# The head of a retention kernel, rewritten by half chunks, with more weight loads issued ahead

## The chip, the cores and the metric

The kernel runs on one core of a Trainium2 chip. The time is device microseconds of one launch. The core's engines run beside each other, each its own instructions in their written order: TensorE (PE, matrix products), VectorE (DVE), ScalarE (ACT), GpSimd (POOL, idle here) and SyncE (SP), which issues DMAs.

## The reference

```python
scores = scale * np.matmul(q, k.transpose(0, 1, 3, 2))      # 4 batches, 8 heads, 576 tokens, 64 wide
gamma = 1.0 - 2.0 ** (-5.0 - np.arange(H, dtype=np.float32))
Dmat = np.where(rel >= 0, gamma[:, None, None] ** rel[None, :, :], 0.0)
x = np.matmul(scores * Dmat[None, :, :, :], v)              # then to 2304 tokens x 512
h = x @ w_in;  g = np.maximum(h, 0) + np.log1p(np.exp(-np.abs(h)));  x = g @ w_out     # 512 -> 2048 -> 512
h = x @ w2_in; r = np.maximum(h, 0); out = (r * r) @ w2_out
```

All in float32. The decay is split into factors of the key's token (multiplied into v) and of the query's token (the table xw, multiplied into the result), so that only a triangular mask of zeros and ones is left, and everything before a chunk is one 64x64 state per head.

## The kernel before, in words

**Chunks.** The 2304 tokens are 18 chunks of 128, each two half chunks of 64 tokens; 9 half chunks are one batch, and the state begins anew with each batch. Per half chunk: scores k times q, a mask, the output from the masked scores and from the carried state, and the state's own sum.

**Layers.** The two matrix layers work on tiles of 512 or 384 tokens. Each weight matrix of the first pair is cut into 16 slices of 128 hidden units ("wi" of w_in, "wo" of w_out). A raw slice (512 KB, loaded into one of three stage buffers by `load_w`) is turned into words (`words`: two ScalarE instructions, L152 and L153, then two of VectorE, L157 and L160) and split into a high part (ScalarE's cast, L188) and a low part (VectorE's subtraction, L189). A product is three passes: high by high, low by high, high by low. `pump_load(upto)` issues loads up to a number, `pump_begin` starts slices, `pump_end` finishes them one step later.

**The head.** Lines 1136 to 1219 are written in an order by hand ("manual schedule"), and each engine keeps it. They compute attention for the first four chunks (tile 0), the factor tables xw for half chunks 1 to 8 (sent as one row, spread by TensorE in `spread_rows`, multiplied by VectorE in `make_xw` and by ScalarE in `scalar_xw`, four instructions per half chunk), and the first weight slices. In the kernel before, a chunk's queries and keys come in two loads, heads 0 to 3 into partitions 0 to 63 and heads 4 to 7 into the others (`early_qk`), and both half chunks are worked on together, over 128 tokens: `early_scores` makes 128x128 scores, `early_mask` masks 1024 columns, `early_states` adds all 128 tokens, and one copy of the state (`kept`) carries it to the next chunk. `early_x` multiplies by xw (x), and ScalarE's cast and `early_low` split x. `early_g1` is the first-layer product of slice 0 in two column halves. Slice 0 is finished in the head; slices 1 and 2 have their words made there and are split in step 0.

**The steps after it.** Step j does the first-layer product of slice j (L515), softplus, one visit of the attention (`visit`: scores L391, states L416, outputs L439, masks L401, the scaling of v L372), the split of its result (L533, L534), the second-layer product of slice j-2 (L549), and starts two more slices. The visits of steps 0 and 1 are scores alone: chunk 3 was finished by the head, and the first half of chunk 4 is the last of its batch, whose state nobody needs. Step 2 begins with outputs that need the mask of step 1, step 3 with states that need the values scaled in step 2. Attention chunks from the fifth on sit in a ring of two buffers (`ring`), loaded as whole rows of 4 KB in all 128 partitions.

**Warming.** `keep_warm(n)` gives TensorE n products of zeros, of two instructions each.

## Time and profile before

| | |
|---|---|
| median of 3 runs | 826.17 us (826.15 to 827.8) |
| the profiled execution | 823.74 us |
| its span, first to last instruction | 822.0 us |
| mean granted TensorE clock | 0.997 |
| busy: TensorE, VectorE, ScalarE | 810.8 (99%), 607.2 (74%), 378.9 us (46%) |
| DMA | 189.37 MB, mean 230 GB/s |

The profile has a page with busy times, forty slices, DMA queues and the chain that ended last, and views of the trace behind it: windows (busy time in stretches), the chain of waits, timelines of one engine, and DMA issues with their time to landing. "Idle before" is the time an engine stood before an instruction, followed by what released it. A product in float32 is recorded as two instructions. In a timeline neighbouring instructions of one kind are one row.

### The profile page before, as it was taken

The page shows a single profiled execution, that of the slowest core. Times are in us where ns is not written, and L with a number is a line of the kernel's source. Part 1 is how long each engine was busy: PE and PEld are TensorE (multiplying, and loading weights), DVE is VectorE, ACT ScalarE, POOL GpSimd, SP SyncE. Part 2 cuts the span into 40 slices and gives each one's busy share as a digit, 9 for nine tenths or more (in the row PEclk, how much of TensorE's full clock was granted, in tenths as well). Part 3 has the DMA queues.
Part 4 walks back from the last instruction along what each step waited for, and adds up shares of the span by engine and source line. Part 5 has one row for each costly group of instructions (what it writes and reads, how often), then busy time and mean ns, then how long its engine had stood idle before and what let it go on. Part 6 is the DMA issues. An engine that isn't in the chain of part 4 may idle for free.

```text
span 822.0 us, 16243 instructions
## 1 busy us (share of the span) xinstructions
PE 810.8 (99%) x5957; PEld 721.6 (88%) x5957; DVE 607.2 (74%) x1160; ACT 378.9 (46%) x739; POOL 0.2 (0%) x4
## 2 busy tenths in 40 slices
PE   8898999999999999999999999999999999999998
PEld 5777999988888888888999999988999988999887
DVE  4998766646565664646796498998798997787876
ACT  3787666535344543545665221454211554111553
POOL 0000000000000000000000000000000000000000
PEclk9999999999999999999999999999999999999999
DMA  9967554466666655656979387898978889888885
GB/s 238 310 219 239 180 180 124 134 207 215 209 229 213 194 172 188 197 181 211 300 251 300 94 251 248 271 297 285 299 249 254 250 271 282 282 249 249 251 274 170
DMA packets 122802, 189.37 MB, mean 230 GB/s; under 512 B 10466, under 2 KB 68450, under 8 KB 122722
## 3 DMA queue, kind: packets, MB, share of 16 engines
q1 hardware_dynamic: 122560, 188.26, 72.1%
q8 instruction: 47, 0.77, 0.4%
q14 instruction: 31, 0.25, 0.1%
q10 hardware_dynamic: 164, 0.09, 0.1%
HBM read 147.41 MB, written 40.89 MB: 229 GB/s over the span
## 4 chain that ended last, share of the span: by engine, by line
PE 95%; DMA 3%; DVE 1%; ACT 0%; SPq 0%; issue 0%; DVEq 0%; ACTq 0%
PE acc L549 24%; PE ph L515 24%; PE py L685 9%; PE py L758 9%; PE px L685 6%; PE pz L758 6%; PE px L758 6%; PE pz L685 6%; PE po L439 2%; DMA qk<-in_qk_t_dram 1%; PE pb L391 1%; PE st L416 1%; DMA kv<-in_kv_dram 1%; DMA ring<-in_qk_t_dram 1%; SPq L970 0%
## 5 line engine op out<-in xcount | busy, mean ns | idle before, releaser
L515 PE MATMUL ph<-xh,wi 128*128 128x512 f32 (+1 forms) x632 | 144.4, 370 | 1.3 <-DVE wi L189 0.8
L515 PEld LDWEIGHTS ph<-xh,wi 128*128 128x128 f32 x632 | 115.9, 189 | 17.0 <-DVE wi L189 1.2
L549 PE MATMUL acc<-gh,woh 128*128 128x512 f32 (+1 forms) x320 | 120.5, 377 | 0.0
L549 PE MATMUL acc<-gh,wol 128*128 128x512 f32 (+1 forms) x320 | 117.8, 368 | 0.0
L549 PE MATMUL acc<-gl,woh 128*128 128x512 f32 (+1 forms) x320 | 117.8, 368 | 0.0
L534 DVE TENSOR_TENSOR gl<-e,gh 128x512 fp32r<-128x512 f32 (+1 forms) x80 | 51.0, 637 | 71.1 <-ACT gh L533 70.3
L526 ACT ACTIVATE e<-ph 128x512 f32<-128x512 f32 (+1 forms) x80 | 44.3, 554 | 126.4 <-PE ph L515 126.2
L685 PE MATMUL py<-t,sring 128*128 128x384 f32 x432 | 88.3, 338 | 0.0
L515 PE MATMUL ph<-xl,wi 128*128 128x512 f32 (+1 forms) x316 | 78.2, 369 | 0.0
L685 PEld LDWEIGHTS py<-t,sring 128*128 128x128 f32 x432 | 74.8, 188 | 2.5 <-DVE uring L889 0.5
L549 PEld LDWEIGHTS acc<-gh,woh 128*128 128x128 f32 x320 | 60.0, 188 | 8.6
L549 PEld LDWEIGHTS acc<-gh,wol 128*128 128x128 f32 x320 | 60.1, 188 | 7.7
L549 PEld LDWEIGHTS acc<-gl,woh 128*128 128x128 f32 x320 | 60.1, 188 | 6.9
L515 PEld LDWEIGHTS ph<-xl,wi 128*128 128x128 f32 x316 | 58.5, 190 | 7.6
L738 ACT CAST gh<-g 128x384 fp32r<-128x384 f32 x84 | 43.2, 515 | 46.2 <-PE px L758 16.1
L738 ACT CAST gring<-g 128x384 fp32r<-128x384 f32 x84 | 43.2, 515 | 39.9 <-PE py L758 16.2
L685 PE MATMUL pz<-t,sring 128*128 128x384 f32 x288 | 58.3, 334 | 0.0
L685 PE MATMUL px<-t,sring 128*128 128x384 f32 x288 | 58.0, 335 | 0.0
L401 DVE TENSOR_TENSOR ring<-pb,cst 64x256 f32<-64x256 f32 x56 | 23.6, 422 | 44.1 <-PE pb L391 27.2
L706 DVE TENSOR_TENSOR g<-g 128x384 f32<-128x384 f32 x96 | 52.6, 554 | 1.5
L706 DVE TENSOR_TENSOR gring<-g,gring 128x384 fp32r<-128x384 f32 x84 | 46.2, 553 | 9.5 <-ACT gring L738 8.3
L706 DVE TENSOR_TENSOR gl<-g,gh 128x384 fp32r<-128x384 f32 x84 | 46.5, 554 | 8.8 <-ACT gh L738 7.7
(123 smaller groups left out, 1403.2 us busy)
## 6 DMA issues: line engine op xcount, KB each, us to landing
sring<-s2d SPq DMA_DIRECT2D x168, 256.0 KB, 3.1
sring<-o2d SPq DMA_DIRECT2D x168, 256.0 KB, 3.2
wi_raw<-in_moe_w_in_dram SPq DMA_DIRECT2D x32, 512.0 KB, 4.9
wo_raw<-in_moe_w_out_dram SPq DMA_DIRECT2D x32, 512.0 KB, 4.1
s2d<-ct SPq DMA_DIRECT2D x48, 256.0 KB, 2.8
o2d<-ct SPq DMA_DIRECT2D x48, 256.0 KB, 3.4
ring<-in_qk_t_dram SPq DMA_DIRECT2D x14, 512.0 KB, 4.1
ring<-in_kv_dram SPq DMA_DIRECT2D x14, 512.0 KB, 6.3
```

The lines of the kernel that those rows point to most:

```text
L391: nc.tensor.matmul(pb[to, h, :], lhsT=kk[:, hh, :], rhs=qp[:, hh, :], start=True, stop=True, skip_group_check=True,)
L401: nc.vector.tensor_tensor(out=chunk[c][rows, 1, i * HH:(i + 1) * HH], in0=pb[of], in1=mask[of], op=ALU.mult)
L416: nc.tensor.matmul(st[to, h, :], lhsT=kk[:, hh, :], rhs=sv[:, hh, :], start=m == h == 0, stop=True, skip_group_check=True,)
L439: nc.tensor.matmul(po[(LO, HI)[hh % 2], hh // 2, :], lhsT=before[rows, hh, :] if carried else sv[:, hh, :], rhs=qp[:, hh, :] if carried el ...
L515: nc.tensor.matmul(ph[:, :n], lhsT=a, rhs=x, start=(j == 0), stop=(j == len(todo) - 1))
L526: nc.scalar.activation(out=g, in_=hps.pop(key)[:, :n], func=AF.Softplus)
L534: nc.vector.tensor_tensor(out=l[:, :n], in0=g, in1=h[:, :n], op=ALU.subtract)
L549: nc.tensor.matmul(acc[j][:, :n], lhsT=a, rhs=x, start=(begin and m == 0), stop=(end and m == 2))
L685: nc.tensor.matmul(ps, lhsT=a, rhs=x, start=(first and m == 0), stop=(m == len(todo) - 1), skip_group_check=True,)
L706: nc.vector.tensor_tensor(out=out, in0=a, in1=b, op=ALU.subtract)
L738: nc.scalar.copy(h, src)
L758: nc.tensor.matmul(blocks[m][:, :cols], lhsT=a[:, c], rhs=x, start=(first and p == n == 0), stop=(p == NP - 1 and n == len(todo) - 1), ski ...
```

## The change

The head is written anew. Queries and keys of the first four chunks come like those of the ring, as whole rows of 4 KB in all partitions, one load per pair (q and k; k and v). Scores, states and outputs are made per half chunk, by the functions that the later visits use; scores and masks cover 64x64 blocks, so a chunk's mask has 512 columns. The state is carried after each half chunk, by `next_state`, into one of two buffers. The table rows move from ScalarE's to SyncE's DMA queue. The warming products are two, not six, and the single one after `spread_rows` goes. Weight slice 0 is loaded before chunks 2 and 3, and three more raw slices get buffers of their own (`ahead`, in the place of a later slice group), so that six are loaded in the head. Slice 1 is split in the head; slice 2's words are made there.

```diff
+EXTRA = 3
+    ahead = wts.tile([P, EXTRA, DM, 2], U32, tag="wi2", name="ahead")
     def load_w(src, kind, f):
-        t = stage.tile([P, DM, 2], U32, tag="st", name=f"{kind}_raw")
+        if STAGES <= n_load[0] < STAGES + EXTRA:
+            t = ahead[:, n_load[0] - STAGES]
+        else:
+            t = stage.tile([P, DM, 2], U32, tag="st", name=f"{kind}_raw")
...
     def pump_load(upto):
+        if upto >= STAGES:
+            upto = min(upto + EXTRA, max(2 * STAGES + EXTRA, upto))
...
+    def early_load(c, i):
+        if c not in chunk:
+            chunk[c] = first_pool.tile([P, 4, H, CN], F32, tag=f"chunk{c}", name="chunk", bufs=1)
+        nc.sync.dma_start(
+            out=chunk[c][:, i:i + 2],
+            in_=(qk_t, None, kv)[i][2 * c:2 * c + 2].rearrange("s p i h c -> (s p) i h c"),
+        )
     def early_scores(c):
+        pb = ps_head.tile([P, H, CN], F32, tag="pb", name="pb", bufs=2)
+        for hh in range(H):
+            for rows in (LO, HI):
+                nc.tensor.matmul(
+                    pb[rows, hh, :], lhsT=chunk[c][rows, 1, hh, :], rhs=chunk[c][rows, 0, hh, :],
+                    start=True, stop=True, skip_group_check=True,
+                )
+        return pb
+    def early_mask(c, pb):
+        nc.vector.tensor_tensor(out=chunk[c][:, 1], in0=pb, in1=whole_mask, op=ALU.mult)
+    carried = [
+        first_pool.tile([P, H, CN], F32, tag=f"carried{i}", name="carried", bufs=1)
+        for i in range(2)
+    ] * (last // 2) + [before]
+    def early_state(c, s):
+        for fn in states(c, s):
+            fn()
+    def early_next(c, s):
+        next_state(c, s, carried[c + s])
+    def early_outputs(c):
+        po = pos[c] = ps_head.tile([P, 2, 512], F32, tag="po", name="po", bufs=1)
+        both = (
+            outputs(c, s, po[:, s].rearrange("p (a n) -> p a n", n=CN), False, carried[c])
+            for s in range(2)
+        )
+        rounds(*(at_rounds((0, fns)) for fns in both))
...
+        early_load(0, 0)
         for half in (LO, HI):
             nc.scalar.dma_start(out=cst[half, :C_XW], in_=consts[CN:P, :C_XW])
+        early_load(0, 2)
+            nc.sync.dma_start(out=rows_in[r:r + 1], in_=consts[r:r + 1, C_XW:])
+        early_load(1, 0)
+        early_load(1, 2)
+        pump_load(1)
+        early_load(2, 0)
+        early_load(2, 2)
+        early_load(3, 0)
+        early_load(3, 2)
+        for _ in range(2):
+            load_w(*loads[n_load[0]])
+            n_load[0] += 1
         load_chunk(last)
+        pump_load(STAGES)
-        keep_warm(6)
+        keep_warm(2)
+        pb0 = early_scores(0)
+        scale_v(0)
+        early_mask(0, pb0)
+        early_state(0, 0)
+        early_next(0, 0)
+        pb1 = early_scores(1)
+        scale_v(1)
+        early_state(0, 1)
+        early_mask(1, pb1)
+        early_next(0, 1)
         spread_rows()
-        keep_warm(1)
...
+        early_state(1, 1)
+        early_next(1, 1)
+        make_xw(2, 2)
+        scalar_xw(4)
+        early_x(0)
+        pb2 = early_scores(2)
+        scale_v(2)
+        early_mask(2, pb2)
+        early_state(2, 0)
+        early_next(2, 0)
+        scalar_xw(5)
+        early_low(0)
+        early_outputs(1)
+        early_state(2, 1)
+        early_next(2, 1)
+        scalar_xw(6)
+        words0 = begin_words()
+        scale_v(3)
+        early_keep(0)
+        pb3 = early_scores(3)
+        early_x(1)
+        early_state(3, 0)
+        early_next(3, 0)
+        scalar_xw(7)
+        early_mask(3, pb3)
+        next(words0)
+        early_outputs(2)
+        early_state(3, 1)
+        early_x(2)
+        early_low(1)
+        early_keep(1)
+        next(words0)
+        early_outputs(3)
+        early_x(3)
+        early_low(2)
+        early_keep(2)
+        early_next(3, 1)
+        scalar_xw(8)
+        words1 = begin_words()
+        early_low(3)
+        early_keep(3)
         early_g1(0)
+        next(words1)
+        next(words1)
+        words2 = begin_words()
+        next(words2)
```

## Rows read from the trace of the kernel before

**Rows 1.** The page, part 4: shares of the span on the chain that ended last.
```profile
PE 95%; DMA 3%; DVE 1%; ACT 0%; SPq 0%; issue 0%; DVEq 0%; ACTq 0%
```

**Rows 2.** Chain of waits, 0 to 60 us: start, length, what (us).
```profile
9.58 9.78 DMA qk<-in_qk_t_dram
...
31.64 4.38 PE ph L515 x11
```

**Rows 3.** Windows: stretch, its length, busy us (instructions) by engine, TensorE's clock, DMA share, GB/s.
```profile
7.00:8.00 1.00, 1.00 (x4) 0.38 (x2) 0.00 (x0) 0.00 (x0) 0.00 (x0) 1.00 1.12 208
...
24.00:25.00 1.00, 1.00 (x24) 0.85 (x16) 0.90 (x3) 0.19 (x2) 0.00 (x0) 1.00 1.05 402
...
0.00:26.00 26.00, 22.46 (x329) 14.66 (x330) 14.85 (x29) 11.92 (x33) 0.20 (x4) 1.00 0.97 266
...
2.00:4.00 2.00, 2.00 (x3) 0.67 (x2) 0.19 (x1) 0.97 (x1) 0.00 (x0) 1.00 0.80 211
...
30.00:35.00 5.00, 3.86 (x10) 2.87 (x11) 4.65 (x9) 2.80 (x5) 0.00 (x0) 0.72 0.94 315
```

**Rows 4.** Timeline of TensorE, 28 to 47 us: start, us, instruction, [idle before, releaser].
```profile
29.20 0.68 PE L391 MATMUL pb<-ring 64*64 64x64 f32 x16
...
30.29 0.50 PE L515 MATMUL ph<-xh,wi 128*128 128x512 f32 x1 [0.41 <-ACT wi L188]
...
31.64 2.94 PE L515 MATMUL ph<-xh,wi 128*128 128x512 f32 x7 [0.85 <-DVE wi L189]
...
34.37 1.65 PE L515 MATMUL ph<-xl,wi 128*128 128x512 f32 x4
...
38.52 1.07 PE L515 MATMUL ph<-xl,wi 128*128 128x512 f32 x4
...
39.51 0.27 PE L439 MATMUL po<-ring 64*64 64x64 f32 x2
...
46.40 0.27 PE L416 MATMUL st<-ring 64*64 64x64 f32 x2
```

**Rows 5.** DMA issues at 17.8 and 31.4 us: KB each, us from issue to landing.
```profile
ring<-in_kv_dram SPq DMA_DIRECT2D x1, 512.0 KB, 10.1
...
ring<-in_qk_t_dram SPq DMA_DIRECT2D x1, 512.0 KB, 6.4
```

**Rows 6.** Timeline of SyncE's queue, 14 to 18.5 us.
```profile
17.77 0.77 SPq L362 DMA_DIRECT2D ring<-in_kv_dram  x1
```

**Rows 7.** Timeline of VectorE, 9 to 45 us.
```profile
9.65 1.22 DVE L1013 TENSOR_TENSOR mixed<-pb,causal 128x1024 f32<-128x1024 f32 x1 [3.97 <-PE pb L992]
...
25.59 0.69 DVE L189 TENSOR_TENSOR wi<-ct,wi 128x512 fp32r<-128x512 f32 x1
...
28.18 0.69 DVE L157 SCALAR_TENSOR_TENSOR wi_raw<-wi_raw 128x512 f32<-128x512 f32 x1
...
28.90 0.69 DVE L160 SCALAR_TENSOR_TENSOR ct<-wi_raw 128x512 uint32<-128x512 uint32 x1
...
32.38 0.86 DVE L401 TENSOR_TENSOR ring<-pb,cst 64x256 f32<-64x256 f32 x2
...
36.68 0.86 DVE L401 TENSOR_TENSOR ring<-pb,cst 64x256 f32<-64x256 f32 x2
...
44.29 0.68 DVE L372 TENSOR_TENSOR ring<-ring,vw 128x512 f32<-128x512 f32 x1
```

**Rows 8.** Timeline of ScalarE, 19 to 28 us.
```profile
19.58 2.02 ACT L1131 ACTIVATE cst<-cst,times 128x64 f32<-128x64 f32 x8
...
24.94 0.62 ACT L188 CAST wi<-ct 128x512 fp32r<-128x512 f32 x1 [0.81 <-DVE ct L160]
...
25.46 0.69 ACT L152 ACTIVATE wi_raw<-wi_raw 128x512 f32<-128x512 f32 x1
...
26.04 0.75 ACT L153 ACTIVATE wi_raw<-wi_raw,cst 128x512 uint32<-128x512 uint16 x1
...
27.44 0.74 ACT L427 COPY ring<-st 64x256 f32<-64x256 f32 x2
```

## Prediction, made before the changed kernel had run

> **What bounds the kernel now.** I read the page first: the chain that ended last is 95% TensorE [rows 1], so over the whole span only what delays TensorE counts. The change touches the first 35 us alone, so the next view was the chain of that stretch. Until 19.4 us it is input DMA (the fourth query-key load was issued at 9.58 and took 9.78 us to land) [rows 2]. The windows say why: in 7 to 8 us, where almost only query-key halves move, DMA gave 208 GB/s; in 24 to 25 us, where a chunk is loaded as whole rows, 402 GB/s [rows 3]. From 30 to 35 us VectorE is busy 4.65 of 5 us, and TensorE stands twice (0.41 and 0.85 us) for the high and low parts of weight slice 1, then runs at a mean granted clock of 0.72 [rows 3, 4]. [...] So the head ends where VectorE and ScalarE have prepared weight slices 1 and 2 and the attention masks of steps 0 to 2. When TensorE restarts, and how far VectorE runs ahead of it then, decides. All later work is the same in both kernels, in the same order, and nothing in it waits for a fixed time, so a shift there reaches the end.

> **Input DMA (gain).** Up to and with the third chunk's key-value rows, the new order has seven loads of 524 KB (one weight slice among them), 69 KB of constants and 18 KB of factor rows: 3.76 MB. All but the weight slice and the factor rows now spread over 128 partitions in 4 KB rows. Bounds for their rate are 208 GB/s (halves) and 402 (whole rows); the nearest row is the whole-row one, and I take 380. Bytes begin to move at about 2.3 us (211 GB/s over 2 to 4 us is 0.42 MB) [rows 3]. A landing lags its last byte: 26.0 us at 266 GB/s make the 6.92 MB up to and with the first ring chunk's key-value rows, which were issued at 17.77 and took 10.1, so landed at 27.9; I take 1.8 us [rows 3, 5, 6]. Third chunk's key-value: 2.3 + 3.76/0.38 + 1.8 = 14.0 us; fourth, 1.05 MB later, 16.8. In the old kernel even the fourth query-key load came at 19.36 [rows 2]. At 300 GB/s the 14.0 becomes 16.6, at 402 it becomes 13.5, at 208 22.2.

> **What VectorE loses.** Masks of 128x1024 (1.22 us each) become 128x512; by the 128x512 products of other lines 0.68 each [rows 7], so four times 0.54, 2.2 us less. Scaling, the tables and the weight words cost what they did.

> **What ScalarE gains.** Each chunk now carries its state twice, in two 64x256 copies (0.74 a carry) [rows 8]. Seven carries come into the head, 5.2 us, for three single copies, which by the same row can't be under 0.37 each: some 4 us more. And the carries are serial: a state is added to only when it is copied out.

> **The sum: a serial chain on two engines.** From the third chunk on, each engine's next instruction waits for the other's. ScalarE's instructions overlap by 0.1 (starts 25.46 and 26.04, the first 0.69 long), so I count a carry 0.65, four factor tables 1.0 (2.02 for eight), a slice's words 1.25 (0.69 + 0.75), a cast 0.52, each 0.1 more where VectorE waits for its end [rows 8]; VectorE's words of a slice are 1.45, its subtraction or product 0.69 [rows 7].
> - 14.0, scaling 0.68, states 0.68 as eight 64x64 products on TensorE [rows 4]: 15.4.
> - ScalarE, without a gap: carry, tables of block 5, carry, tables 6, words of slice 0, cast of x1, carry, tables 7: 0.65+1.0+0.65+1.0+1.25+0.52+0.65+1.0 = 6.7: 22.1.
> - Cast of x2 0.52 and of slice 0 0.62; VectorE's low part 0.69 and x3 0.68: 24.6.
> - ScalarE: cast of x3 0.52, last carry 0.65, tables 8 1.0, words of slice 1 1.35: 28.1. VectorE's words 1.45: 29.6.
> - ScalarE: cast of slice 1 0.52, words of slice 2 1.35; VectorE's words 1.45; cast 0.62; low part 0.69: 34.2.
> - A dozen hand-overs at 0.05 (a cast of 0.62 that began at 24.94 released VectorE at 25.59) [rows 7, 8]: 34.8.

> There VectorE begins the mask of step 0, which stands at 32.38 in the old kernel [rows 7]: 2.4 us later, although its input came earlier. The old order gave ScalarE the words of slices 1 and 2 while VectorE still had x work of its own; the new one leaves VectorE idle at nearly every link (some 6 us in all).

> TensorE had room for part of this. The outputs of step 2 began at 39.51 and need the mask of step 1, which ended at 37.54; 2.4 later is 39.94: 0.4 us late. The states of step 3 began at 46.40 and need values scaled by 44.97; 2.4 later is 47.4, against 46.8: 0.6 more [rows 4, 7]. From there TensorE has no gap to give back. Sum so far: **+1.0 us**.

> **The clock.** Six warming products become two, and the one between goes too. The warming ran at three instructions in 2 to 4 us and at four in 7 to 8 alone [rows 3], so at half speed at first. The new TensorE ends warming near 4 us, does 0.7 us of scores and then stands until the first values are scaled, near 8. What the clock does then no row of before shows; the nearest is 30 to 35 us, where gaps of 0.41 and 0.85 us were followed by half speed (four products 1.65 us against 1.07) [rows 3, 4]. If states, scores and outputs run at half speed from 8 to 12 us, the second carry of chunk 1 and the tables behind it come up to 2.5 us late, of which the wait for the third chunk covers part. Bounds 0 and 2.5; I take +0.5. Later, TensorE stands about 2.9 us before slice 1 is ready (its restart falls near 31.4). The half-speed product that follows lies beside VectorE's lateness; what comes out past 40 us costs 0 to 1.5 (the loss of the old dip: 4.38 us times 1 - 1.07/1.65) [rows 2, 4]; I take +0.5.

> [...]

> **Six loads ahead.** They bring the first second-layer slice earlier, which VectorE's lateness covers anyway: 0. The loads after them, and the fifth ring chunk behind these on SyncE's queue, wait until slice 2's words are done (near 33.1): issue 33.5, landing near 40 with the 6.4 us that its query-key rows took before [rows 5], wanted just after 39.9. I take 0, bounds 0 and 0.5. Factor rows on SyncE's queue cost a microsecond of issue while a megabyte is queued: 0. The distance of the later loads stays.

> **Forecast.** +1.0 +0.5 +0.5 = +2.0 us. The profiled execution took 823.74 (span 822.0) and would take 825.7; the median of the runs shown, 826.17, stands 2.43 above it, so I predict **828.2**. About 0.2% (1.65 us) can be told from no change.

> **Rivals.**
> - *Half speed through the whole head.* [...] States, scores and outputs then take twice their time: 2.5 us up to the third chunk's first carry, 0.6 at the second, 0.9 at the last outputs, 4.0 on top of +1.0: 831.2. Chance 0.16.
> - *No clock cost, input at 402 GB/s.* The chain starts at 13.5, step 0's mask at 34.3: by the same two slacks TensorE is 0.5 late, 826.7, not to be told from no change. Chance 0.32.
> - *Faster: VectorE's saved work decides, not ScalarE.* If ScalarE is done before VectorE asks at each step, VectorE runs densely from the fourth chunk's landing: eight products and subtractions (5.5), three slices' words (4.35), two more low parts (1.4) and hand-overs (0.4), 16.8 + 11.6 = 28.4, 4.0 earlier than 32.38. TensorE then loses its gaps (1.26) and the dip (1.5): -2.8, 823.4. It decides from the point where ScalarE's 6.7 us end before 20 us; by the sum they end at 22.1. Chance 0.10.
> - The forecast itself, slower by 1.7 to 4 us: 0.42.

> Faster 0.10, same 0.32, slower 0.42 + 0.16 = 0.58. Range: below, the second rival with 0.9 of slack in my hand-overs and overlaps (825.8); above, the clock rival and half a microsecond for the ring chunk (831.8), which also holds a landing at 300 GB/s. The likeliest's own range is 827.8 to 830.2.

> **What would show it.** In the new trace: key-value landings near 14 and 17 us and DMA above 350 GB/s before 15 us (input); ScalarE without idle time from 15.5 to 22, and VectorE idle for about 2 us before the words of slice 1 (chain); step 0's mask on VectorE at 34 to 36; TensorE idle for about 3 us before the second first-layer product, released by the low part of slice 1; a granted clock below 1 between 8 and 12 us and again between 30 and 40. I am wrong if slice 1 is ready before 30 us, if the landings are as late as before, or if TensorE's outputs of step 2 begin before 39.51 [rows 4].

## The result and the profile after

The changed kernel takes 831.52 us (median of 4 runs, 830.85 to 831.88), the kernel before 826.78 beside it: a ratio of 1.0055 with a 95% interval of 1.0038 to 1.0073, some 4.7 us slower. The forecast was 828.2: the sign is right, the time lies at the upper end of the range, and the loss is more than twice what I gave it. The profiled execution took 831.65 us with a span of 829.8.

Kernels are compared by ratios, since the median of the kernel before moved between 826.0 and 827.7 from one comparison to the next. Its profiled execution in front of the prediction, 823.74, was one of its better ones; another profile of it comes under the experiments.

The windows of the changed kernel (columns as in [rows 3]):

```profile
5.00:10.00 5.00, 3.00 (x70) 2.70 (x71) 1.97 (x6) 0.67 (x2) 0.00 (x0) 0.92 0.99 341
10.00:15.00 5.00, 5.00 (x101) 4.44 (x99) 2.13 (x4) 2.00 (x7) 0.00 (x0) 0.50 1.03 407
15.00:20.00 5.00, 5.00 (x149) 5.00 (x147) 3.18 (x5) 3.56 (x12) 0.00 (x0) 0.55 1.06 374
20.00:25.00 5.00, 3.43 (x133) 3.04 (x131) 3.02 (x5) 4.90 (x15) 0.00 (x0) 1.00 1.04 381
25.00:30.00 5.00, 2.14 (x80) 1.80 (x77) 1.99 (x4) 1.78 (x6) 0.00 (x0) 0.97 0.52 156
30.00:35.00 5.00, 4.86 (x40) 4.58 (x39) 3.11 (x5) 3.61 (x10) 0.00 (x0) 0.69 0.57 161
```

The input does what it should: 341 to 407 GB/s. TensorE runs at half its clock from 9.2 to 19.4 us (granted clock 0.50 and 0.55 in the two windows that hold most of it). Then something no term named: between 25 and 30 us all three engines are mostly idle (2.14, 1.99 and 1.78 of 5 us), with the clock back at full (0.97).

The chain of waits of the changed kernel says who was waited for there (start, length, what):

```profile
21.53 1.54 issue
23.07 0.62 PE st L423 x14
...
26.23 2.76 issue
28.99 0.73 PE po L446 x31
29.74 0.70 DVE x L1023
30.46 0.62 ACT xh L1028
```

"issue" is a wait for nothing that the profile shows. Two such waits, 4.3 us together, lie on the chain. TensorE's timeline (answers to [rows 4]):

```profile
23.07 0.62 PE L423 MATMUL st<-chunk 64*64 64x64 f32 x14 [1.54 <-issue]
...
28.99 0.69 PE L446 MATMUL po<-chunk,carried 64*64 64x64 f32 x31 [2.76 <-issue]
...
35.61 0.49 PE L522 MATMUL ph<-xh,wi 128*128 128x512 f32 x1 [0.76 <-ACT wi L193]
36.34 1.90 PE L522 MATMUL ph<-xh,wi 128*128 128x512 f32 x7 [0.23 <-DVE wi L194]
...
40.08 0.68 PE L398 MATMUL pb<-ring 64*64 64x64 f32 x16 [0.90 <-DVE ring L408]
...
44.35 0.27 PE L446 MATMUL po<-ring 64*64 64x64 f32 x2 [0.65 <-DVE ring L408]
```

Both stops fall inside a group of like products whose first ones had already run on the same tiles. VectorE and ScalarE pass them on (answers to [rows 7, 8]):

```profile
24.75 0.69 DVE L1023 TENSOR_TENSOR x<-po,cst 128x512 f32<-128x512 f32 x1 [0.51 <-PE po L446]
...
29.74 0.69 DVE L1023 TENSOR_TENSOR x<-po,cst 128x512 f32<-128x512 f32 x1 [2.24 <-PE po L446]
33.42 0.69 DVE L162 SCALAR_TENSOR_TENSOR wi_raw<-wi_raw 128x512 f32<-128x512 f32 x1 [1.61 <-ACT wi_raw L157]
...
39.08 0.86 DVE L408 TENSOR_TENSOR ring<-pb,cst 64x256 f32<-64x256 f32 x2
...
43.35 0.85 DVE L408 TENSOR_TENSOR ring<-pb,cst 64x256 f32<-64x256 f32 x2
```

```profile
18.62 0.74 ACT L434 COPY carried<-st 64x256 f32<-64x256 f32 x2
...
30.46 0.62 ACT L1028 CAST xh<-x 128x512 fp32r<-128x512 f32 x1 [3.69 <-DVE x L1023]
...
32.73 0.66 ACT L157 ACTIVATE wi_raw<-wi_raw 128x512 f32<-128x512 f32 x1
```

The x of the head's last chunk starts at 29.74, the words of slice 1 follow, and step 0's mask stands at 39.08, 6.7 us later than in [rows 7]. The outputs of step 2 begin at 44.35, 4.84 after the 39.51 of [rows 4]; the span is 7.8 longer than that of the profile before.

**What the stops are.** Count TensorE's recorded instructions (products and weight loads, a float32 product being two of each, and drains and waits for semaphores, 361 of them in the whole kernel) in order of start. The stops stand before numbers 705 and 961 (counted from 0), 256 apart. The instruction queue of the DMA (q8 of the page: 49 packets, 0.80 MB) moves packets of 16 KB; in the head they start at 13.76, 20.66, 26.71 and 30.04 us, and TensorE goes on 2.4 us after the second (23.07) and 2.3 after the third (28.99). The queue moved 49 such packets in the changed kernel and 47 in the kernel before, near 1/256 of the recorded instructions (49.4 and 48.0). So the reading, an inference from these counts and times, is that each packet brings TensorE a block of 256 instructions, and that TensorE had run out of them twice, for 1.54 and 2.76 us. The new head has 363 more recorded instructions than the old (12639 against 12276 in the whole kernel; 248 float32 products of attention against 152 in the head, since half chunks need more and smaller ones). In both profiles of the kernel before, no stop of TensorE from 10 to 40 us is longer than 0.98 us, and none stands at these numbers: with fewer and larger products the 256 from number 449 on last there from 19.91 to 28.76 us (profile before the prediction), longer than the 6.9 and 6.05 us between the first three packets here.

### The profile page after: what moved, and what is told of

Read it like the earlier page. It is cut to its first block, busy times and chain, and to the rows that moved or that the text cites. A ratio compares the mean times of both kernels' runs of the same rounds, so it can differ in the third digit from the quotient of the medians.

```text
span 829.8 us, 16610 instructions
## 1 busy us (share of the span) xinstructions
PE 810.4 (98%) x6139; PEld 725.4 (87%) x6139; DVE 605.6 (73%) x1154; ACT 382.9 (46%) x750; POOL 0.2 (0%) x4
## 4 chain that ended last, share of the span: by engine, by line
PE 87%; DVE 5%; DMA 4%; issue 2%; ACT 2%; SPq 0%; ACTq 0%; DVEq 0%
PE acc L556 21%; PE ph L522 19%; PE py L692 9%; PE py L765 9%; PE px L692 6%; PE pz L765 6%; PE px L765 6%; PE pz L692 6%; PE po L446 2%; PE st L423 1%; DVE ct L165 1%; DMA ring<-x2d 1%; DMA ring<-in_qk_t_dram 1%; PE pb L398 1%; DMA cst<-in_consts_dram 1%
## 5 line engine op out<-in xcount | busy, mean ns | idle before, releaser
L745 ACT CAST gring<-g 128x384 fp32r<-128x384 f32 x84 | 43.2, 515 | 39.9 <-PE py L765 16.2
L713 DVE TENSOR_TENSOR gl<-g,gh 128x384 fp32r<-128x384 f32 x84 | 46.8, 559 | 8.8 <-ACT gh L745 7.7
```

Of the source, the lines that this page charges most:

```text
L713: nc.vector.tensor_tensor(out=out, in0=a, in1=b, op=ALU.subtract)
L745: nc.scalar.copy(h, src)
```

## The experiments

Three theories: **supply** (TensorE's instructions come too slowly), **clock** (the half-speed stretch), **order** (the words of slices 1 and 2 stand last on ScalarE). "Mask" is the start of step 0's mask on VectorE in the profiled execution, "last x" that of x of chunk 3. The ratio is the one on record; it is not the quotient of the two medians, which differs from it by up to 0.0024 (e10: 834.02 over 827.69, 1.0076; e5: 828.85 over 826.01, 1.0034).

| kernel | ratio to before (95%) | last x | mask |
|---|---|---|---|
| before, second profile (e4) | 1.0000 (0.9985–1.0015) | 27.38 | 33.55 |
| changed | 1.0055 (1.0038–1.0073) | 29.74 | 39.08 |
| e1 six warming products | 1.0063 (1.0049–1.0077) | 29.08 | 38.39 |
| e2 no loads ahead | 1.0044 (1.0029–1.0059) | 27.74 | 37.05 |
| e3 words first | 1.0041 (1.0022–1.0059) | 30.09 | 35.68 |
| e5 no carried products | 1.0014 (0.9995–1.0032) | 25.59 | 34.92 |
| e6 late loads | 1.0048 (1.0028–1.0068) | 27.96 | 37.27 |
| e7 late loads, words first | 1.0027 (1.0009–1.0045) | 30.34 | 35.95 |
| e8 e7 with six warming products | 1.0035 (1.0020–1.0051) | 30.10 | 35.70 |
| e9 e5 with idle products in their place | 1.0090 (1.0074–1.0107) | 29.35 | 38.70 |
| e10 32 idle products more | 1.0100 (1.0081–1.0120) | 30.59 | 39.90 |
| e11 before, loads ahead | 1.0005 (0.9991–1.0020) | 26.75 | 32.93 |
| e12 before, two warming products | 1.0000 (0.9985–1.0014) | 26.77 | 32.95 |

**e1, the clock.**
```diff
-        keep_warm(2)
+        keep_warm(6)
```

> The changed kernel with six warming products instead of two (the single one after the table rows stays out). Clock theory: the half-speed stretch from 9 to 19 us goes, the first carry of chunk 2 on ScalarE moves from 18.6 to about 16 us, and the kernel gains 2 to 2.5 us on the changed one (about 829.2). Supply theory: TensorE's instructions come in blocks of 256 and a block takes up to 5.9 us while DMA is backlogged; then the carry is earlier, but TensorE still stops twice, 256 recorded instructions apart, and the gain is 1 us or less. Order theory (only the serial chain of ScalarE and VectorE counts): no more than 0.5 us.

The clock was full from 6.5 to 23.5 us and at half for 3.4 us behind that (granted clock 1.00 in the windows from 5 to 20 us, 0.85 and 0.81 in the next two; in the changed kernel 13.7 us at half between 9.2 and 33.1), and nothing was gained. TensorE's timeline of this run shows why:

```profile
17.00 0.33 PE L985 MATMUL pb<-chunk 64*64 64x64 f32 x4 [0.82 <-issue]
...
23.29 0.33 PE L985 MATMUL pb<-chunk 64*64 64x64 f32 x5 [3.27 <-issue]
...
28.22 0.28 PE L446 MATMUL po<-chunk 64*64 64x64 f32 x4 [0.59 <-issue]
```

A faster TensorE reached the end of its blocks sooner and stood longer in sum (4.7 us against 4.3), before numbers 449, 705 and 961. A part of the missing gain is the price of the remedy: six warming products last until 9.27 us, and the first states start at 10.14 instead of 8.59. That is made up by the third carry (13.98, in the changed kernel 13.96). From there the full clock brought TensorE to the end of its block 1.5 us earlier (number 704 starts at 19.81, there at 21.27), and the stop took all of it: number 705 starts at 23.29, there at 23.07. So the clock isn't the deciding cause: what half speed takes up to 19 us, the supply would have taken.

**e2, fewer transfers in the head.**
```diff
-EXTRA = 3
+EXTRA = 0
```
(with the buffer `ahead` left out)

> The changed kernel without the three extra raw slices (EXTRA = 0, no buffer for them), so DMA has 1.57 MB less to move and its backlog ends near 22 us instead of 26. Supply theory: the stop of 2.76 us in the outputs of chunk 3 (26.2 to 29.0) shrinks below 1 us, since its instruction block is fetched at once; the stop of 1.54 us before it stays; VectorE's x of chunk 3 moves from 29.7 to about 27.5 and the kernel gains about 2 us. Clock and order theories: the stop has nothing to do with the loads, no change within 0.5 us; the wait for the first second-layer slice may even cost 0.3.

The stop before number 961 is gone (1.64 and 1.90 us are left, before 449 and 705) and the last x comes 2.0 us earlier, as supply said; the time's interval overlaps the changed kernel's, so the gain in time is not established.

**e3, the order.**
```diff
+        words1 = begin_words()
         early_outputs(3)
+        next(words1)
+        next(words1)
         early_x(3)
...
+        words2 = begin_words()
         scalar_xw(8)
...
```
(the old places of these lines, behind `scalar_xw(8)` and `early_g1(0)`, go)

> The changed kernel with the words and the split of slice 1 put ahead of x of chunk 3, and the words of slice 2 ahead of the tables of block 8. Order theory: the work fills the 3.7 us in which ScalarE stands before 30.5 us, VectorE's mask of step 0 moves from 39.1 to about 35.5, and the kernel gains 3 to 3.5 us (about 828.2). If the clock or the instruction supply alone set the end of the head, the masks would follow TensorE: under 1 us.

The mask came 3.4 us earlier, though the last x came 0.35 later, since VectorE now makes the words before it, and though TensorE stood 0.72, 2.84 and 1.34 us. So order and supply are two causes, and the words of slice 1 behind the last x cost VectorE 3.4 us; in time the intervals overlap.

**e4, the kernel before again.**

> The kernel before, unchanged, as a control with a profile of its own. All theories: the same time within 0.2%. What its head shows beside the first profile tells how far the first one, which was 2.4 us under the median of its runs, stands for the others: either a part of the head (the granted clock, a wait for instructions) differs by 2 to 3 us, or the difference lies outside the head.

Its profile has a span of 825.2 and the mask at 33.55. Against this profile the changed head is 5.5 us late at the mask, 5.25 at the outputs of step 2 (39.10 here) and 4.6 in the span: the lateness of the head is the loss.

**e5, fewer products.**
```diff
-            outputs(..., False, carried[c])
+            outputs(..., False, carried[c])[:HH]
```

> The changed kernel without the products of query and carried state in the head's outputs (left out for chunks 0 to 3; the carries are still copied): 224 of TensorE's recorded instructions fewer before the first-layer product. Supply theory: the boundaries at the 705th and 961st recorded instruction come later in the work, the stop in the outputs of chunk 3 goes, VectorE's x of chunk 3 moves from 29.7 to 27 us or earlier, and the kernel gains 2 us or more on the changed one. Order theory (ScalarE and VectorE set x of chunk 3): the same carries and tables stand in ScalarE's way, under 1 us.

Left out are the products of query and carried state in the head's outputs. With 224 recorded instructions fewer the last x came at 25.59, the mask 4.2 us earlier, and the ratio can't be told from 1. No stop put down to "issue" is longer than 0.4 us; the longest, 1.89 at 22.88, is for ScalarE's copy of a state. Without the products TensorE doesn't wait for those carried states in the outputs either, so e9 had to part the two.

**e6 to e8, later loads, and combinations.** e6 issues slices 1 and 2, the first ring chunk and the loads ahead one by one behind `early_keep(0)` to `early_keep(2)`:
```diff
         early_keep(0)
+        for _ in range(2):
+            load_w(*loads[n_load[0]])
+            n_load[0] += 1
...
         early_keep(1)
+        load_chunk(last)
...
         early_keep(2)
+        pump_load(STAGES)
```
(the lines that issued them at the head's start go; e7 has e6's and e3's edits, e8 those and six warming products)

> The changed kernel with the same loads, but those of slices 1 and 2 issued behind the store of x0, the first ring chunk behind that of x1 and the three extra slices behind that of x2, so that DMA is not backlogged between 16 and 26 us. Supply theory: an instruction block then arrives some 3.3 us after TensorE asks for it instead of 5.6 to 5.9; both stops together (4.3 us in the changed kernel) shrink to under 1.5, x of chunk 3 comes at 26 to 27.5 us and the kernel gains 2 to 3 us. Order theory: no gain, and slices 1 and 2 land later, so a loss is possible.

> Both remedies: the loads spread as in the run before and the words of slices 1 and 2 drawn ahead as in the third experiment. If the supply of instructions and the order are separate terms, their gains add: VectorE's mask of step 0 at 33 us or earlier (39.1 in the changed kernel, 35.7 with the words alone, 32.4 in the kernel before), and the time within 0.2% of the kernel before (about 826 to 827.5). If they are one and the same, no better than the words alone (35.7, about 829.5).

> As the run before, with six warming products. With the instruction supply out of the way the clock could count: if the early half-speed stretch matters then, the first carry of chunk 2 comes near 16 us and the mask of step 0 another 1 to 2 us earlier (31 to 32, about 825.5). If not, the same as the run before within 0.5 us.

For the times of a block expected of e6 the changed kernel's trace has this: 5.50 us between numbers 449 and 705 (17.57 to 23.07) and 5.92 between 705 and 961 (28.99). The next packet started 1.05 us after 961, and TensorE had gone on 2.3 us after the start of the one before; the 3.3 us are an estimate from these two.

In e6 no stop without a releaser is left; TensorE waits for ScalarE instead, 1.7 us for a carried state and 1.9 for the high part of slice 1, and the mask comes at 37.27. But e6 ran at half speed from 10 to 15 us (granted clock 0.50), and its DMA engines were half idle from 15 to 20 (share 0.45): a slower user and a faster supply (the packet for the next block started 1.5 us after number 449, in the changed kernel 3.1). The gain of 2 to 3 us didn't show. In e7, with the same loads and full clock to 20 us (1.00), stops of 1.45 and 2.29 us came back at 449 and 705. Neither combination is told apart from e3: the causes hide each other. Late loads don't mend the supply for a TensorE at full clock, the gains of e3 and e6 didn't add up to a mask at 33, and no combination beats the kernel before.

**e9, number or wait.** Each of e5's missing products is replaced by one on zeros into an unused part of the same bank:
```diff
...
+            fns[:HH] + [lambda s=s: dummies(s, (LO, HI)[s]) for _ in fns[HH:]]
...
```

> The changed kernel in which each product of a carried state in the head's outputs is replaced by a product of the same size on zeros into an unused part of the same PSUM bank: as many TensorE instructions as the changed kernel, none of them waiting for a carried state (so the carried states are left out of the head's outputs, as in the run without these products: 828.85 us, the last x of the head at 25.59 us, the mask of step 0 at 34.92). Theory 'supply of instructions': number and work of the products cost, not the wait for the states: stops between the 448th and 449th, 704th and 705th, and 960th and 961st recorded instruction as in the changed kernel, last x at 28.5 to 30, mask of step 0 at 37.5 to 39.5, time 830.5 to 832. Rival 'waits for the states' (ScalarE's copies come late): last x at 25.5 to 26.5, mask of step 0 at 35, time 828.9 as without the products.

These products wait for nothing and give nothing. TensorE's timeline:

```profile
16.47 1.01 PE L423 MATMUL st<-chunk 64*64 64x64 f32 x14 [2.00 <-issue]
...
22.67 0.72 PE L423 MATMUL st<-chunk 64*64 64x64 f32 x14 [1.67 <-issue]
...
28.60 0.69 PE L1015 MATMUL po<-warm 64*64 64x64 f32 x31 [1.66 <-issue]
```

All three stops are back, before 449, 705 and 961, and last x and mask stand where supply put them. The wait for the states is not it. The three stops, 5.3 us together, are longer than the 3.8 us by which the last x lies behind that of e5, so the products' own work need not have cost anything; e10 bears on this again. In time e9 lies 0.76% above e5, more than I expected.

**e10, number or place.**
```diff
         pb0 = early_scores(0)
+        for _ in range(32):
+            nc.tensor.matmul(cold[LO, :CN], lhsT=warm[LO, :CN], rhs=warm[LO, CN:P], ...)
```

> The changed kernel with 32 more small products (64x64, on zeros) behind the scores of chunk 0, where TensorE is idle for 2.0 us: 128 more recorded instructions before the rest of the head. Theory 'supply': the stops stand at the same numbers (449, 705, 961, and perhaps 1217) and so 128 instructions earlier in the work: behind what are the 320th, 576th and 832nd instruction of the changed kernel. Rival 'the stops belong to places of the program': they move along to the numbers 833 and 1089. The time: 829.5 to 832 by the first (as many stops, at other places), 831.5 by the second.

TensorE's timeline:

```profile
6.71 3.83 PE L1119 MATMUL cold<-warm 64*64 64x64 f32 x63
...
21.50 0.70 PE L446 MATMUL po<-chunk,carried 64*64 64x64 f32 x15 [3.17 <-issue]
...
27.57 0.46 PE L446 MATMUL po<-chunk,carried 64*64 64x64 f32 x15 [0.93 <-issue]
```

Again before numbers 705 and 961, that is 128 instructions earlier in the work, in other groups of products. The stops belong to the count. The 32 products also took 3.8 us, more than the 2.0 of idle time, so the first states came at 10.33 instead of 8.59. Under full clock that was made up by the fifth carry (18.24, in the changed kernel 18.62); the sixth, behind the stop before 705, came 2.6 us later than there (23.10 against 20.47). That fits the count and not the work of the products; but the clock, too, was at half from 20.1 us on (0.51 from 20 to 25 us), so its share isn't parted from that of the stop. The kernel was slower than the changed one and than either theory said: 1.0100 against 1.0055, with intervals that don't meet.

**e11 and e12, parts of the change alone in the kernel before.**
```diff
...
+        if STAGES <= n_load[0] < STAGES + EXTRA:
+            t = ahead[:, n_load[0] - STAGES]
...
```
(with the buffer and `pump_load` of the change)
```diff
-        keep_warm(6)
+        keep_warm(2)
...
-        keep_warm(1)
```

> The kernel before with one part of the change alone: the six weight loads ahead (three tiles of their own, their issues behind the first chunk of the main part). In the changed kernel taking this part away gave 830.12 against 831.52 us with overlapping intervals. If the loads ahead cost by themselves (1.5 MB more of transfers before 30 us, instruction blocks behind them): 827.5 to 829 us. If they cost only together with the new head: within 0.1% of 826.5.

> The kernel before with one part of the change alone: two warming products in place of six and one. Clock theory (half speed behind an idle start costs 0.5 to 2.5 us): the granted clock falls below 1 between 8 and 20 us, 827 to 829 us. Rival 'the clock of the head is hidden' (putting six back into the changed kernel gave full clock and no gain): within 0.1% of 826.5 whatever the clock in the head.

Neither moves the time. In e12 the windows give a clock of 1.00 from 5 us on, but the trace's first record of the clock stands at 16.93 us, and windows before a first record print 1.00. The rows show half speed up to there. Groups of 30 or 32 like score products in e12:

```profile
11.15 1.98 PE L992 MATMUL pb<-qk 64*64 64x128 f32 x30 [0.72 <-DMA qk<-in_qk_t_dram]
...
19.60 1.10 PE L992 MATMUL pb<-qk 64*64 64x128 f32 x32
```

and the one of chunk 1 in e4:

```profile
12.06 1.10 PE L992 MATMUL pb<-qk 64*64 64x128 f32 x30 [0.59 <-DMA qk<-in_qk_t_dram]
```

So half speed up to about 17 us cost the old head nothing that can be measured (mask at 32.95, in e4 33.55), as the rival "hidden" said. Neither part costs by itself; what costs is the rewriting by half chunks with its order. That the loads ahead add to it in the new head is not excluded (e2's mask stands 2.0 us earlier).

## Why the prediction was right in sign and short in size

- **Input DMA: right, and the head was late all the same, as said.** 407 GB/s between 10 and 15 us; the third chunk's key-value rows, issued at 7.53, landed 6.2 us later (13.7, forecast 14.0), and from that chunk on the scaling no longer waited for DMA.
- **The serial chain on two engines: the direction right, its first half mis-sized.** It was to bring the x of chunk 3 to an end at 24.6; it ended at 30.43, 5.8 us later. Two things were missing. The first carry of chunk 2 was put at 15.4 and began at 18.62, behind a TensorE at half speed (in e3, the same head up to there, clock 1.00 to 20 us and 0.58 in the next window, it began at 16.16); the clock term had put 0.5 of its bound of 2.5 us on this. Behind it came two stops of 4.3 us together for instructions, which no term held; by the difference, 1.7 of these 7.5 us fell beside waits that the chain had anyway. The second half was over-sized: from the end of x3 to the mask 10.2 us forecast, 8.65 measured, since VectorE's first word instruction needs only ScalarE's first of a slice, not both. So VectorE's 2.4 us became 6.7, of which e3 takes back 3.4 by order alone.
- **TensorE's slack: right for the profile it was read from, and that profile was generous.** Before the outputs of step 2 it was read as 2.0 us (37.54 to 39.51); the mask of step 1 came 6.67 us later (43.35 against 36.68) and the outputs 4.84, so 1.8 of it was used. But the first profile has most of this gap because its TensorE was at half clock near 34 us (0.72 over 30 to 35 us); in e4, at full clock there (1.00), the mask of step 1 ends at 38.67 and the outputs begin at 39.10, a gap of 0.4. At 44.35 (0.65 us) TensorE stands for this mask. I overlooked that the scores of step 1 write the one PSUM buffer from which step 0's mask reads: at 40.08 (0.90 us) TensorE stands for that mask.
- **The clock: shape right, price not borne out.** Half speed came (9.2 to 19.4 and 29.7 to 33.1 us), but full clock in e1 gained nothing, and half speed up to about 17 us in e12 cost the old head nothing. The granted clock of 1.00 in the row over the first 26 us of the old kernel [rows 3] has no record before 4.87 us behind it. The rival that gave 831.2 by half speed through the whole head came closest to the time, for a cause that e1 refutes as the deciding one; no run shows the half speed through the whole head that its 4.0 us assume, the changed kernel showed 13.7 us of it before 33.1. That 831.52 still lies in the range is luck: its upper end, 831.8, came from this rival.
- **The rival without a clock cost** (mask at 34.3, 826.7) falls with the mask at 39.08.
- **Six loads ahead at 0:** nothing established against it in time (e11 1.0005, and e2's interval overlaps), though e2's mask stands 2.0 us earlier without them.
- **The rival "VectorE's saved work decides"** falls: VectorE waited for TensorE (2.24 us at 29.74) and for ScalarE (1.61 at 33.42).
- **The signs.** Landings and clock as listed; ScalarE was without idle time from 16.37 to 26.77, a microsecond after the 15.5 named; VectorE's wait before the words of slice 1 was 1.61 of about 2 us; the mask at 39.08 missed 34 to 36. TensorE's wait of about 3 us before the second first-layer product was 0.76 and 0.23, because TensorE itself was late by then.

Open: why e9 and e10 lost more in time than at the mask (by the spans of their profiles 2.7 and 1.7 us against the changed kernel); how the loss divides between supply and order when each is mended alone, since their intervals overlap; and why the clock fell early in some of these heads and late in others.

## What to carry to other kernels

Count instructions as well as columns: here 248 smaller float32 products in the place of 152 emptied TensorE's supply for 1.54 us, with the DMA engines full (share 1.04 from 20 to 25 us), and for 2.76 us behind that (0.52 from 25 to 30); in e6, with a share of 0.45 from 15 to 20 us and TensorE at half speed from 10 to 15 (0.50), no such stop was left. A stop released by "issue" in the middle of a group of like products, with another 256 recorded instructions further on, was the sign of it; a faster clock then went into longer stops (e1: 4.7 us against 4.3). A clock of 1.00 before the trace's first clock record is no measurement (e12: 30 products took 1.98 us under a printed 1.00, 32 took 1.10 later): compare how long like instructions take. A gap read from one profile can belong to that execution alone (before the outputs of step 2, 2.0 us in the first profile and 0.4 in e4). Before a wait is priced against an engine's slack, look which PSUM bank or buffer the next product writes, and who still reads it (here 0.90 us, at 40.08).
